# Two-input work on GpSimd and VectorE in planned turns, weight sums on VectorE, one decay operation per batch row

## The chip, the cores and the metric

The kernel runs on one core of a Trainium2 chip. The core has five engines that run on their own instruction queues, each strictly in order: TensorE (PE in the profile, with its weight loads as PEld), VectorE (DVE), ScalarE (ACT), GpSimd (POOL) and SyncE (SP, which here only issues DMAs). They wait for each other through semaphores. [...] The metric is the device time of one execution in microseconds (us), given as the median of several runs. The profile is of one further execution.

## The reference

A gated linear attention is followed by a mixture of four experts, all of which see every token:

```python
B, H, S, D = 4, 8, 768, 48
f = 1.0 / (1.0 + np.exp(-f_logit))
for t in range(S):
    state = f[:, :, t, :, None] * state + np.einsum('bhd,bhe->bhde', k[:, :, t], v[:, :, t])
    y[:, :, t] = np.einsum('bhd,bhde->bhe', q[:, :, t], state)
x = y.transpose(0, 2, 1, 3).reshape(B * S, H * D)              # 3072 x 384
p = domain_probs / (domain_probs.sum(-1, keepdims=True) + 1e-09)
for e in range(4):                                             # w1: 384 x 1024, w2: 1024 x 384
    h = np.maximum(x @ w1[e], 0.0)
    out += p[:, e:e + 1] * (h @ w2[e])
```

## The kernel before

**Tiling.** The 768 steps are cut into six chunks `c` of 128 (0 to 5), each with four batch rows `b`, so a chunk is 512 tokens. In names, "q 3.1" is the step `q` of chunk 3, batch row 1; "relu 2.0.6.0" is chunk 2, expert 0, slice 6 of the 1024 hidden columns, from token column 0.

**Attention of a chunk.** The gates' logarithms are summed along the chunk by a matmul. ScalarE takes two exponentials of the sums (`exps`, into a tile `e`; there are two such tiles). `product` (L298) multiplies q and k with them into a tile `qk`: on VectorE for the first chunks, on GpSimd from chunk 1, batch row 2 on. A transposing DMA (or, early, PE) makes `QK` of it; PE multiplies to scores `A`, VectorE masks them (`ev_at`, L338: one input in PSUM, the mask in SBUF), PE makes `y`. `cast_v` (L303) casts v for it, mostly on GpSimd. Between chunks a state is carried: VectorE adds PE's product to `Sf` (`ev_kv`, L362), and `state` (L364) on GpSimd multiplies `Sf` by the chunk's decay `egs` and casts the result to `Sb`. The state lies in two bands of 48 partitions (0 to 47 and 64 to 111), one for each head of a pair; the partitions between the two hold zero. From chunk 1 on `egs` is fetched by a DMA that GpSimd's queue issues (L296), reading from the last row of tile `e`; this tile is free for a next chunk's `exps` when this DMA and both products have read it.

**Experts.** y, scaled by the expert's probability from chunk 2 on (`ev_x`, ScalarE L318 or VectorE L320), is transposed by DMA to `xT`. PE makes h (L386), ScalarE or VectorE applies the relu while it leaves PSUM (`relu`, L395 and L397). In chunks 0 and 1, PE multiplies h with w2 (L401), and VectorE adds the experts up (`ev_o`, L408). From chunk 2 on the second product is made by two experts at a time and in blocks of two by two, with seven products instead of eight (`p1` to `p7`, L447). For this, four block sums of each h are needed, s1 to s4 (`h_sum`, L435, 128 x 1024 bf16, all on VectorE; s3 overwrites a block of h), and four block differences of each w2 (`w_sum`, L424, 128 x 768 bf16, j = 0 to 3; j = 1 overwrites a block of w2, so an expert's `w_sum` comes after the last plain product with its w2, in chunk 1). Before the change experts 0, 2 and 3 have theirs on GpSimd and expert 1 on VectorE. The seven products are combined in SBUF (`add_c`, L454): first with what PSUM holds, then sums of two SBUF tiles (`plus`, L683), on VectorE or GpSimd.

**What sets the order.** The program's order on every engine is written by a planner, `Plan.run` (L59). Each step has engines on which it may run with a cost in us, a priority, steps it depends on, and buffers it takes and frees. The planner walks through time, gives each free engine the ready step with the first priority, and lists the steps in the order of their planned starts; this list is then emitted. So any change to a cost or to a rule moves steps on all engines, and moves some between engines (a relu between ScalarE and VectorE, for example). On the chip the order on each engine is fixed, while the time of each step is what the semaphores allow.

## Time and profile before

| | |
|---|---|
| median of 3 runs | 317.05 us (315.5 to 317.67) |
| profiled execution, its own time | 315.88 us |
| its span, first to last instruction | 313.9 us |
| mean granted TensorE clock | 0.974 |
| PE busy | 283.7 us (90% of the span) |
| VectorE busy | 206.2 us (66%) |
| ScalarE busy | 182.9 us (58%) |
| GpSimd busy | 141.9 us (45%) |

The span leaves 2.0 us of the profiled execution outside of it. An instruction counts as busy from its start to its end, so the time in which it has started and cannot go on is in it too. The granted clock is the share of TensorE's full clock that the chip allows at that time. Rows with "gap" or "[... <-X]" say how long an engine was idle and what ended this.

### The profile page before, as it was taken

The numbers are of one execution on the slowest core, as the hardware profiler recorded it, in microseconds if no ns is written. First come the engines' busy times: TensorE is split into PE (matmuls) and PEld (weight loads), VectorE is DVE, ScalarE is ACT, GpSimd is POOL, SyncE is SP. The second block draws the span as 40 slices with busy tenths as digits, with TensorE's granted clock in tenths as the row PEclk, the third lists the DMA queues.
The fourth block names the chain that finished last, engine by engine and source line by source line (L and its number), as shares of the span: only waits on it lengthen the run. The fifth ranks groups of instructions, "written<-read, shape, count | busy, mean of one in ns | idle before, by whom it ended". The sixth has DMA issues, their size and how long they took to land.

```text
span 313.9 us, 6483 instructions
## 1 busy us (share of the span) xinstructions
PE 283.7 (90%) x2519; PEld 195.3 (62%) x2548; DVE 206.2 (66%) x340; ACT 182.9 (58%) x347; POOL 141.9 (45%) x199
## 2 busy tenths in 40 slices
PE   6999999999988799923999998998899997999993
PEld 2566555677766564413777766767567766667693
DVE  3874025864653676999789698587998377450363
ACT  5766737476746558820668486757556661656520
POOL 3877102291858919994087463653960001010012
PEclk9999999999999979995899999999999999999998
DMA  8999999969895978990287999796444424110002
GB/s 157 192 190 208 205 206 187 207 164 172 160 202 111 170 145 140 232 199 16 56 160 145 211 204 159 144 146 88 82 94 106 80 18 84 45 58 0 2 12 90
DMA packets 157330, 41.20 MB, mean 131 GB/s; under 512 B 145756, under 2 KB 156508, under 8 KB 157300
## 3 DMA queue, kind: packets, MB, share of 16 engines
q1 hardware_dynamic: 146052, 34.07, 58.0%
q0 software_dynamic: 11248, 6.72, 14.8%
q8 instruction: 20, 0.33, 0.5%
q14 instruction: 10, 0.08, 0.1%
HBM read 31.51 MB, written 4.72 MB: 115 GB/s over the span
## 4 chain that ended last, share of the span: by engine, by line
PE 47%; DMA 20%; DVE 10%; POOL 10%; issue 7%; ACT 3%; SPq 2%; DVEq 0%; POOLq 0%; ACTq 0%
PE ps L386 21%; PE ps L447 19%; DMA w_sb<-in_moe_w_dram 10%; DVE s L435 4%; POOL qk L299 4%; PE ps L401 4%; DMA k<-in_k_dram 3%; DMA xT<-yb 3%; DVE h L435 2%; SPq L234 2%; POOL w_sb L243 2%; ACT yb L318 2%; DVE yb L320 2%; DMA QK<-qk 2%; DMA egs<-e 1%
## 5 line engine op out<-in xcount | busy, mean ns | idle before, releaser
L386 PE MATMUL ps<-xT,w_sb 128*128 128x512 bf16 (+3 forms) x679 | 142.3, 339 | 2.3 <-DVE Sf L362 0.4
L397 ACT ACTIVATE h<-ps 128x512 bf16<-128x512 f32 (+2 forms) x182 | 97.0, 544 | 54.9 <-PE ps L386 50.5
L386 PEld LDWEIGHTS <-w_sb 128*128 128x128 bf16 x708 | 65.8, 98 | 47.0 <-issue 1.0
L447 PEld LDWEIGHTS <-h 128*128 128x128 bf16 x512 | 43.9, 99 | 18.9 <-issue 11.3
L401 PE MATMUL ps<-w_sb,h 128*128 128x384 bf16 x256 | 51.4, 331 | 2.2 <-ACT e L291 1.8
L454 POOL TENSOR_TENSOR o<-o,o 128x384 f32<-128x384 f32 x8 | 8.3, 1044 | 72.1 <-DVE o L454 41.3
L369 POOL TENSOR_TENSOR Sf<-Sf,egs 48x192 f32<-48x192 f32 x40 | 21.8, 545 | 38.7 <-DVE Sf L362 24.8
L447 PEld LDWEIGHTS <-s 128*128 128x128 bf16 x384 | 32.2, 98 | 6.3 <-DVE s L435 2.0
L401 PEld LDWEIGHTS <-h 128*128 128x128 bf16 x256 | 24.8, 99 | 17.8 <-issue 2.8
L447 PE MATMUL ps<-w_sb,h 128*128 128x192 bf16 x256 | 24.8, 253 | 12.1 <-DVE h L395 12.1
L395 DVE TENSOR_SCALAR h<-ps 128x256 bf16<-128x256 f32 (+2 forms) x46 | 24.3, 545 | 15.9 <-PE ps L386 15.2
L291 ACT ACTIVATE e<-ps 128x384 f32<-128x384 f32 x48 | 26.9, 666 | 11.0 <-DMA egs<-e 3.7
L338 DVE TENSOR_TENSOR AT<-ps,mask 128x512 bf16<-128x512 f32 x48 | 30.3, 683 | 3.2 <-PE ps L334 3.2
L408 DVE SCALAR_TENSOR_TENSOR o<-ps,pn,o 128x384 f32<-128x384 f32 x24 | 14.6, 615 | 26.7 <-PE ps L401 26.2
L435 DVE TENSOR_TENSOR s<-h 128x1024 bf16<-128x1024 bf16 x16 | 18.7, 1168 | 16.7 <-ACT h L397 16.6
L320 DVE TENSOR_SCALAR yb<-ps,pn 128x384 bf16<-128x384 f32 x27 | 16.4, 616 | 19.6 <-ACT yb L318 14.2
L299 POOL TENSOR_TENSOR qk<-q,e 128x384 bf16<-128x384 f32 x18 | 22.8, 1270 | 13.4 <-ACT e L291 12.2
L318 ACT ACTIVATE yb<-ps,pn 128x384 bf16<-128x384 f32 x37 | 20.5, 582 | 13.3 <-DVE yb L320 10.4
L299 POOL TENSOR_TENSOR qk<-k,e 128x384 bf16<-128x384 f32 x20 | 22.6, 1135 | 8.7 <-ACT e L291 4.3
L454 DVE TENSOR_TENSOR o<-o,ps 128x384 f32<-128x384 f32 (+1 forms) x36 | 18.8, 538 | 11.2 <-PE ps L447 8.3
L223 ACT COPY o<-ps 128x384 f32<-128x384 f32 x23 | 11.0, 479 | 23.5 <-PE ps L447 23.4
L447 PE MATMUL ps<-w_sb,s 128*128 128x192 bf16 x256 | 23.9, 246 | 0.0
(74 smaller groups left out, 335.4 us busy)
## 6 DMA issues: line engine op xcount, KB each, us to landing
out_dram<-o SPq DMA_DIRECT2D x23, 192.0 KB, 2.0
w_sb<-in_moe_w_dram POOLq DMA_DIRECT2D x5, 768.0 KB, 18.1
k<-in_k_dram SPq DMA_DIRECT2D x10, 384.0 KB, 5.2
q<-in_q_dram SPq DMA_DIRECT2D x10, 384.0 KB, 5.1
v<-in_v_dram SPq DMA_DIRECT2D x10, 384.0 KB, 5.1
f<-in_f_logit_dram SPq DMA_DIRECT2D x9, 384.0 KB, 4.6
w_sb<-in_moe_w_dram POOLq DMA_DIRECT2D x6, 384.0 KB, 8.4
f<-in_f_logit_dram SPq DMA_DIRECT2D x6, 192.0 KB, 3.8
```

The costliest lines, as they stand in the source:

```text
L291: nc.scalar.activation(out=o, in_=i, func=AF.Exp, scale=1.0 if j else -1.0)
L299: engines[eng].tensor_tensor(out=tl("qk", c, b)[:, j, :, 0:D].rearrange("t (i r) d -> t i r d", r=2), in0=tl("qk"[j], c, b // 2)[:, hh(b), ...
L318: nc.scalar.activation(out=out, in_=in_, func=AF.Copy, scale=pe)
L320: nc.vector.tensor_single_scalar(out=out, in_=in_, scalar=pe, op=ALU.mult)
L338: nc.vector.tensor_tensor(out=tl("AT", c, b)[:, r], in0=tl("A", c, b, r), in1=mask01.unsqueeze(1).broadcast_to([T, NP, T]), op=ALU.mult)
L386: nc.tensor.matmul(out=hp(c, e, fc, n0, n1, nf)[:, f], lhsT=w1_sb[:, e, kk, (fc + f) * 128:(fc + f + 1) * 128], rhs=x_of(c, e)[:, kk, n0:n ...
L395: nc.vector.tensor_relu(out=dst, in_=src)
L397: nc.scalar.activation(out=dst, in_=src, func=AF.Relu)
L401: nc.tensor.matmul(out=tl("op", c, e, nt, part)[:, cols], lhsT=tl("h", c, e, half_of(c, nt * T))[:, fc, nt * T:(nt + 1) * T], rhs=w2_sb[:, ...
L435: engines[eng].tensor_tensor(out=o, in0=x, in1=y, op=op)
L447: nc.tensor.matmul(out=tl("pp_", c, g, bank(c, g, r))[:, u], lhsT=a[:, fc, u * T:(u + 1) * T], rhs=w[:, fc], start=(n + fc == 0 and bank(c ...
L454: engines[eng].tensor_tensor(out=o[:, us], in0=x[:, us], in1=y[:, us], op=ALU.add)
```

## The change

Three things are changed.

1. Steps that read SBUF on GpSimd, and steps with two SBUF inputs on VectorE, are marked `port`: the products of chunks 1 to 5, `cast_v`, `state`, `w_sum`, `h_sum`, and the sums of two SBUF tiles (`plus`). The planner starts no marked step on either engine while another marked one is planned to run. Where a marked GpSimd step follows a marked VectorE step in this order, it gets a semaphore wait for it (`behind`); 24 GpSimd steps get one. VectorE gets no wait for GpSimd.
2. All sixteen `w_sum` steps are on VectorE, planned at 0.62 us each; before, twelve were on GpSimd, planned at 1.75 us.
3. `state` makes one decay multiplication over partitions 0 to 111 instead of one for each band; the two casts stay. Its planned cost goes from 1.75 to 1.25 us.

The helpers `copy`, `product`, `cast_v`, `w_sum`, `h_sum`, `add_c` now return the instruction they make, so that a wait can be put on it; line numbers move by three to six.

```diff
@@ Plan.run
+        port, last = 0.0, None
...
-                        if e in o.costs:
+                        if e in o.costs and not (o.port and e in ("DVE", "POOL") and port > now + 1e-9):
...
+                    if o.port and e in ("DVE", "POOL"):
+                        if e == "POOL" and last is not None and last.engine == "DVE":
+                            o.behind = last
+                        port, last = o.end, o
...
-            nexts = [t for t in free_at.values()] + [f[0] for f in freeing]
+            nexts = [t for t in free_at.values()] + [f[0] for f in freeing] + [port]
@@ state
-        egs, nb = tl("egs", c, b)[:, 0:NP], Sb
+        eg = tl("egs", c, b)[0:MP, 0:NP].unsqueeze(2).broadcast_to([MP, NP, D])
+        first = nc.gpsimd.tensor_tensor(out=Sf[:, b], in0=Sf[:, b], in1=eg, op=ALU.mult)
         for r in range(2):
             rows = slice(r * P2, r * P2 + D)
-            eg = egs[rows, :].unsqueeze(2).broadcast_to([D, NP, D])
-            nc.gpsimd.tensor_tensor(out=Sf[rows, b], in0=Sf[rows, b], in1=eg, op=ALU.mult)
-            nc.gpsimd.tensor_copy(out=nb[rows, b, :, r * D:(r + 1) * D], in_=Sf[rows, b])
+            nc.gpsimd.tensor_copy(out=Sb[rows, b, :, r * D:(r + 1) * D], in_=Sf[rows, b])
+        return first
@@ attention (port=c > 0 for the products, port=True for cast_v)
-            kvdone[c, b] = P.add(f"state {c}.{b}", {"POOL": 1.75}, on(state), s15 + 0.2,
-                                 deps=[ek, GS[b]], frees=[("egs", c, b)])
+            kvdone[c, b] = P.add(f"state {c}.{b}", {"POOL": 1.25}, on(state), s15 + 0.2,
+                                 deps=[ek, GS[b]], frees=[("egs", c, b)], port=True)
@@ add_wsum (add_sums and plus: port=True, costs as they were)
-            wsum[e] = P.add(f"w_sum{j} {e}", {"DVE": 0.62} if e == 1 else {"POOL": 1.75}, lambda eg, j=j: w_sum(e, j, eg), unit[0] + 6,
-                            deps=[omm[c, e, nt] for c in range(S0) for nt in range(B)] + [wsum.get(e)])
+            wsum[e] = P.add(f"w_sum{j} {e}", {"DVE": 0.62}, lambda eg, j=j: w_sum(e, j, eg), unit[0] + 6,
+                            deps=[omm[c, e, nt] for c in range(S0) for nt in range(B)] + [wsum.get(e)], port=True)
@@ the emission
-        o.emit(o.engine)
+        o.made = o.emit(o.engine)
+        if o.behind is not None:
+            after(o.made, o.behind.made)
```

The order that the planner makes of it differs at many places. On VectorE, between the last `ev_o` of chunk 1 and the first block sums of chunk 2 (the numbers in the names are buffers; `w_sb` and `tw` are written by the weight sums, `h` by the relus, `s` by the block sums, `yb` by the scaling of y), the order before is:

```order
125 L408 SCALAR_TENSOR_TENSOR o_1472<-ps_1701,pn,o_1472 128x384
126 L408 SCALAR_TENSOR_TENSOR o_1523<-ps_1750,pn,o_1523 128x384
127 L320 TENSOR_SCALAR yb_1831<-ps_1766,pn 128x384
128 L424 TENSOR_TENSOR w_sb<-w_sb 128x4x192
129 L424 TENSOR_TENSOR tw<-w_sb 128x768
130 L408 SCALAR_TENSOR_TENSOR o_1472<-ps_1824,pn,o_1472 128x384
131 L424 TENSOR_TENSOR tw<-w_sb,tw 128x768
132 L408 SCALAR_TENSOR_TENSOR o_1523<-ps_1833,pn,o_1523 128x384
133 L395 TENSOR_SCALAR h_1880<-ps_1910 128x512
134 L395 TENSOR_SCALAR h_1880<-ps_1915 128x512
135 L395 TENSOR_SCALAR h_1935<-ps_1924 128x512
136 L435 TENSOR_TENSOR s_1944<-h_1880 128x1024
```

With the change the same stretch (w_sum is L429 there, the relu L400, the block sum L440) is:

```order
128 L400 TENSOR_SCALAR h_1700<-ps_1807 128x256
129 L429 TENSOR_TENSOR tw<-w_sb 128x768 x2
130 L429 TENSOR_TENSOR w_sb<-w_sb 128x4x192
131 L413 SCALAR_TENSOR_TENSOR o_1465<-ps_1813,pn,o_1465 128x384
132 L413 SCALAR_TENSOR_TENSOR o_1515<-ps_1822,pn,o_1515 128x384
133 L429 TENSOR_TENSOR tw<-w_sb 128x768
134 L429 TENSOR_TENSOR w_sb<-w_sb 128x4x192
135 L429 TENSOR_TENSOR tw<-w_sb,tw 128x768
136 L429 TENSOR_TENSOR tw<-w_sb 128x768 x2
137 L429 TENSOR_TENSOR tw<-w_sb,tw 128x768
138 L400 TENSOR_SCALAR h_1863<-ps_1894 128x512
141 L440 TENSOR_TENSOR s_1937<-h_1863 128x1024
```

Nine weight sums stand ahead of the relu of slice 6 (row 133 before, 138 now), where three stood; between rows 138 and 141 are the two other relus. Two small relus, rows 126 and 128 of the change, have come from ScalarE.

On GpSimd, in the same time, the order before has the products and casts of chunk 3 (`qk`, `vb`), the DMA issues of the decays (`egs`) and the weight sums without a wait for VectorE between them ("Activation", "DMAHW" and "Pool" are semaphores of ScalarE, of a load and of GpSimd itself):

```order
114 L296 DMA egs_1908<-e_100 128x1x4
115 L296 DMA egs_1919<-e_102 128x1x4
116 L424 TENSOR_TENSOR tw<-w_sb 128x768 x2
117 L424 TENSOR_TENSOR w_sb<-w_sb 128x4x192 [waits Pool_49]
118 L299 TENSOR_TENSOR qk_98<-q_1898,e_100 128x8x48 [waits DMAHW7_49,DMAHW1_49,Activation_49]
119 L299 TENSOR_TENSOR qk_98<-k_1878,e_100 128x8x48 [waits DMAHW0_49,Activation_49]
120 L225 CAST vb_2026<-v_1937 128x384 [waits DMAHW3_49]
121 L299 TENSOR_TENSOR qk_90<-q_1898,e_102 128x8x48 [waits Activation_49]
122 L299 TENSOR_TENSOR qk_90<-k_1878,e_102 128x8x48 [waits Activation_49]
123 L225 CAST vb_2082<-v_1937 128x384
```

With the change the products of batch rows 0 and 1 of chunk 3 stand in this form:

```order
91 L301 DMA egs_1838<-e_100 128x1x4 [waits Activation_49]
92 L304 TENSOR_TENSOR qk_94<-q_1696,e_100 128x8x48 [waits DMAHW2_49,DVE_49,Pool_49]
93 L304 TENSOR_TENSOR qk_94<-k_1518,e_100 128x8x48 [waits DMAHW4_49,Activation_49]
94 L301 DMA egs_1870<-e_102 128x1x4 [waits Activation_49]
95 L230 CAST vb_1907<-v_1749 128x384 [waits DMAHW3_49,DVE_49]
96 L304 TENSOR_TENSOR qk_96<-q_1696,e_102 128x8x48 [waits DMAHW6_49]
97 L304 TENSOR_TENSOR qk_96<-k_1518,e_102 128x8x48 [waits Activation_49]
```

The weight sums are gone from it; row 92 waits for the third weight sum on VectorE (row 130 there), row 95 for the ninth (row 137). Later in the queue the cast "v 3.1" waits for s1 2.0, "q 3.2" for s4 2.0 and "k 3.2" for a weight sum of expert 2.

On GpSimd in chunk 2, the DMA issue of the first decay (egs 2.0, row 64) stood ahead of the products before:

```order
64 L296 DMA egs_1207<-e_100 128x1x4 [waits DMASW3_49,Activation_49]
65 L299 TENSOR_TENSOR qk_96<-k_1114,e_100 128x8x48 [waits DMAHW5_49,Activation_49]
66 L299 TENSOR_TENSOR qk_98<-k_1114,e_102 128x8x48 [waits Activation_49]
67 L299 TENSOR_TENSOR qk_96<-q_1145,e_100 128x8x48 [waits DMAHW6_49]
68 L369 TENSOR_TENSOR Sf<-Sf,egs_1081 48x192 [waits DMASW1_49,DVE_49]
69 L370 CAST sb<-Sf 48x4x48 [waits PE_49,Pool_49]
70 L369 TENSOR_TENSOR Sf<-Sf,egs_1081 48x192 [waits DVE_49]
```

With the change it stands at the end of this group, next to the second (egs 2.1, row 70):

```order
59 L371 TENSOR_TENSOR Sf<-Sf,egs_1066 112x192 [waits DMASW1_49,DVE_49]
60 L374 CAST sb<-Sf 48x4x48 [waits PE_49,Pool_49]
61 L374 CAST sb<-Sf 48x4x48
62 L371 TENSOR_TENSOR Sf<-Sf,egs_1079 112x192 [waits DMASW2_49,DVE_49,Pool_49]
63 L374 CAST sb<-Sf 48x4x48 [waits PE_49,Pool_49]
64 L374 CAST sb<-Sf 48x4x48
65 L304 TENSOR_TENSOR qk_96<-q_1137,e_100 128x8x48 [waits DMAHW6_49,Pool_49]
66 L230 CAST vb_1321<-v_1176 128x384 [waits DMAHW7_49]
67 L304 TENSOR_TENSOR qk_98<-q_1137,e_102 128x8x48
68 L230 CAST vb_1353<-v_1176 128x384
69 L301 DMA egs_1356<-e_100 128x1x4 [waits DMASW3_49]
70 L301 DMA egs_1375<-e_102 128x1x4 [waits DMASW4_49]
```

The two states of chunk 1 (rows 68 to 75 before, 59 to 64 now) have gone ahead of the q products, and both decays' fetches come last.

More of the change, by code (lines that the diff above doesn't have):

```diff
@@ L21, in __init__ @@
         self.takes, self.frees, self.lag = list(takes), list(frees), lag
-        self.end = self.start = self.engine = None
+        self.end = self.start = self.engine = self.behind = None
+        self.port = port
         self.pad = 0
@@ L222, in copy @@
         if eng == "ACT":
[L223 to L225 removed]
+            return nc.scalar.copy(out=out, in_=in_)
+        return engines[eng].tensor_copy(out=out, in_=in_)
     def load(c, nm, b, n):
@@ L451, in add_c @@
         if x is None:
-            copy(eng, o[:, us], y[:, us])
-        else:
-            engines[eng].tensor_tensor(out=o[:, us], in0=x[:, us], in1=y[:, us], op=ALU.add)
+            return copy(eng, o[:, us], y[:, us])
+        return engines[eng].tensor_tensor(out=o[:, us], in0=x[:, us], in1=y[:, us], op=ALU.add)
     def store_c(c, i, j, o, us):
```

29 lines of the change are left out of this document (13 added, 16 removed).

## The prediction

> **What bounds the kernel now.** I read the page's slices first, then stretches of 8 us around the gap in them, then the chain of waits through the gap, then the one line that the chain names. On the page, each digit is the busy tenths of a fortieth of the span:
>
> ```profile
> PE   6999999999988799923999998998899997999993
> ```
>
> PE is full nearly everywhere except in slices 18 and 19, and in the tail. Stretches around them (busy us and count per engine, then the granted clock):
>
> ```profile
> core 0: us, PE busy (x) PEld busy (x) DVE busy (x) ACT busy (x) POOL busy (x), PEclk, DMA share, GB/s
> 136.00:144.00 8.00, 0.00 (x0) 0.00 (x0) 8.00 (x2) 0.33 (x1) 7.98 (x8) 0.79 0.78 149
> 144.00:152.00 8.00, 5.54 (x46) 4.33 (x47) 7.97 (x13) 1.25 (x3) 0.42 (x1) 0.57 0.01 2
> 152.00:160.00 8.00, 7.95 (x102) 5.94 (x101) 5.51 (x12) 6.00 (x12) 3.25 (x8) 1.00 0.56 107
> ```
>
> From 136 to 144 PE does nothing, and VectorE is "busy" for 8.00 us with parts of two instructions. The chain of waits (start, us, what) and the list of who waited for whom (us, times, longest) show the connection:
>
> ```profile
> 128.22 6.55 DVE s L435
> 134.80 2.97 DVE s L435
> 137.77 7.21 DVE h L435
> ...
> 146.24 2.71 PE ps L447 x16
> 148.96 0.97 PE ps L334 x16
> ...
> 151.19 1.32 PE ps L447 x16
> 152.51 0.65 PE ps L386 x3
> ...
> 158.85 0.55 PE ps L334 x16
> ```
>
> ```profile
> PE ps L447 <- DVE h L395: 12.1, 2, 10.5
> ```
>
> PE waited 10.5 us for relus that stand on VectorE behind three block sums. Such a sum is short elsewhere (ns, min/median/max):
>
> ```profile
> L435 DVE TENSOR_TENSOR s<-h x16: 677/692/6542, 128.2 to 300.2; 128x1024 bf16<-128x1024 bf16 x16
> ...
> L435 DVE TENSOR_TENSOR h<-h x16: 677/686/7292, 137.7 to 302.0; 128x1024 bf16<-128x1024 bf16 x16
> ```
>
> The maxima are two of the three in the chain. Together these took 6.55 + 2.97 + 7.29 = 16.8 us for work of 3 x 0.69 = 2.1, so 14.7 us of standing. What GpSimd did then, in order of time:
>
> ```profile
> 128.22 3.24 POOL L424 TENSOR_TENSOR tw<-w_sb 128x768 bf16<-128x768 bf16 x2
> 131.41 1.64 POOL L424 TENSOR_TENSOR w_sb<-w_sb 128x768 bf16<-128x768 bf16 x1
> 133.01 1.18 POOL L299 TENSOR_TENSOR qk<-q,e 128x384 bf16<-128x384 f32 x1
> 134.15 1.47 POOL L299 TENSOR_TENSOR qk<-k,e 128x384 bf16<-128x384 f32 x1
> 135.57 0.49 POOL L225 CAST vb<-v 128x384 bf16<-128x384 f32 x1
> ...
> 139.61 1.65 POOL L424 TENSOR_TENSOR tw<-w_sb 128x768 bf16<-128x768 bf16 x1
> ...
> 142.79 1.63 POOL L424 TENSOR_TENSOR tw<-w_sb,tw 128x768 bf16<-128x768 bf16 x1
> ```
>
> A row that starts before the last one's end, as at 134.15, belongs to one train with it. The first sum starts with the train of weight sums at 128.22 and ends at 134.8, only after three of them and the q product. The third ends at 145.0, right after the last weight sum (144.4). So VectorE is shut out while a train lasts, not for one instruction. It gets a turn between a q and a k product: there the k product takes 1.47 us instead of
>
> ```profile
> L299 POOL TENSOR_TENSOR qk<-k,e x20: 988/1012/1465, 6.3 to 230.8; 128x384 bf16<-128x384 f32 x20
> ```
>
> its 1.01.
>
> **The change part by part.** *The hole.* The weight sums leave GpSimd, so the trains that made the hole are gone: 10.5 us of PE idle time. Behind it PE ran at a granted clock of 0.57: sixteen L447 matmuls took 2.71 us against 1.32 at 151.19, and sixteen L334 ones 0.97 against 0.55, so 1.39 + 0.42 = 1.8 us more. Both go if PE does not stop: -12.3.
>
> The Trainium skill ("SBUF — State Buffer", section "Who interferes with whom") says that the pair of SBUF ports that VectorE and GpSimd share is locked for one whole instruction, and that a VectorE instruction with two SBUF inputs meets a GpSimd one that reads SBUF. By that rule three sums lose at most 4.9 us, and the change is worth little (a rival, below). The trace agrees on who collides and not on how long: 14.7 us.
>
> *What VectorE takes over.* Its own three weight sums of before give the price:
>
> ```profile
> 120.04 0.58 DVE L424 TENSOR_TENSOR w_sb<-w_sb 128x768 bf16<-128x768 bf16 x1
> 120.66 0.75 DVE L424 TENSOR_TENSOR tw<-w_sb 128x768 bf16<-128x768 bf16 x1
> ...
> 121.86 0.73 DVE L424 TENSOR_TENSOR tw<-w_sb,tw 128x768 bf16<-128x768 bf16 x1
> ```
>
> Mean 0.69 us. Ahead of the relu of slice 6, nine stand where three stood: 6 x 0.69 = 4.1 us, and two relus of 128x256 from ScalarE at 0.42 (group below): 0.8. VectorE had idled 3.2 us there, waiting for PE:
>
> ```profile
> 118.46 1.14 DVE L408 SCALAR_TENSOR_TENSOR o<-ps,pn,o 128x384 f32<-128x384 f32 x2
> 126.32 1.99 DVE L395 TENSOR_SCALAR h<-ps 128x512 bf16<-128x512 f32 x3 [3.20 <-PE ps L386]
> L395 DVE TENSOR_SCALAR h<-ps 128x256 bf16<-128x256 f32 x24 | 9.8, 422 | 10.2 <-PE ps L386 9.7 <-ACT h L397 0.3
> ```
>
> So the relus come 4.9 - 3.2 = 1.7 us late. Collisions add to it: the q and k products of "q 3.0" start behind the third weight sum and last 1.2 + 1.0 us; two `ev_o` (1.14 us), which read PSUM, cover half, so the next weight sum stands between 0 and 2.2 us; I take 1.0, one turn, because turns pass between products. Up to the score masks of chunk 3, two more weight sums (1.4) come and one relu of 0.66 (1.99 for three) goes: +0.7. Five more follow by the block sums of expert 2: 3.4 us, and VectorE had 2.5 us idle in 152 to 160, so 0 to 3.4 lands on PE; I take 1.0. Together +4.4, between 2.4 (1.7 + 0.7) and 8.0.
>
> *The decay.* 128x384 on GpSimd takes 1.01 us, 48x192 takes 0.50 (the median of the group below), half for half the elements of a partition, so I take 0.5 for 112x192 too; if rows counted, it would be up to 1.0 and nothing gained. A state saves 0.5 and a step of 0.08:
>
> ```profile
> L369 POOL TENSOR_TENSOR Sf<-Sf,egs x40: 495/502/1047, 25.0 to 220.9; 48x192 f32<-48x192 f32 x40
> L296 POOL DMA_DIRECT2D egs<-e x16 | 9.0, 563 | 11.2 <-ACT e L291 11.2
> 89.10 4.56 DMA egs<-e
> 93.76 1.16 ACT L291 ACTIVATE e<-ps 128x384 f32<-128x384 f32 x2 [3.70 <-DMA egs<-e]
> 94.98 0.81 PE L401 MATMUL ps<-w_sb,h 128*128 128x384 bf16 x4 [1.83 <-ACT e L291]
> ```
>
> Here it is on the path: ScalarE waited 3.70 us for the decay's fetch (egs 2.1), relus stood behind, and PE stood 1.83 us. Two states ahead of this issue give 2 x 0.58 = 1.15 us. The issue of egs 2.0 (0.56 us) goes from the front of the group to its end, just ahead of this one; so the whole group starts 0.5 us earlier, egs 2.0 is issued at 89.1 - 1.15 - 0.5 = 87.5, and egs 2.1 at 88.0. But the earlier pair of `exps` waits now for the late egs 2.0, on ScalarE, in front of the same relus: after a fetch of 4.56 us it starts at 92.1, and the second pair ends at 94.3 (1.1 us each) instead of 94.9. I take -0.6, bounds -1.15 and +1.2 (one pair's 1.16 us behind the last landing). The other eighteen states are off the path.
>
> *Later collisions.* In chunk 4, PE waited for a block sum that ran 1.52 us instead of 0.69, beside the product "q 5.0":
>
> ```profile
> 217.46 1.20 POOL L299 TENSOR_TENSOR qk<-q,e 128x384 bf16<-128x384 f32 x1 [0.83 <-POOL sb L370]
> 217.68 1.52 DVE s L435
> PE ps L447 <- DVE s L435: 1.8, 1, 1.8
> ```
>
> "q 5.0" now waits for a later VectorE step: -0.8, bounds 0 and -1.8.
>
> *The waits.* Behind a waiting GpSimd instruction stand products, casts and decay fetches; the transposing DMAs and then PE's scores wait for those. The longest such chain: "k 3.2" waits for a weight sum of expert 2, which VectorE ends at 129.0 (126.3 + 2.7) + five relus 3.3 + eight block sums 5.5 + two weight sums 1.4 = 139.2. "k 3.3" ends 3.7 us behind that (1.0 + 0.5 + 1.2 + 1.0), and a transpose takes up to
>
> ```profile
> 189.70 4.74 DMA QK<-qk
> ```
>
> 4.74 us: 147.6. PE reached these scores (L334) at 158.85, without the hole and its slow clock at 146.5; but they now stand behind five more h groups of 0.65 and one p5 of 1.32: 151.1. Cover of 3.5 us, so 0; without it every us of VectorE's lag counts here again.
>
> Sum: 315.88 - 12.3 + 4.4 - 0.6 - 0.8 = 306.6. The profiled execution lies 1.2 us below the median of the runs, 317.05; I add some of that and say 307.
>
> **The rivals.** *VectorE becomes the bound.* It is 7.97 of 8 us busy behind the hole. If the costs reach their bound of 8.0 and nothing else is gained, the sum is 315.9 - 12.3 + 8.0 = 311.6. For: thirteen more weight sums stand ahead of s4 of expert 2 than in this stretch before. Against: several stand where VectorE was idle. Chance 0.17.
>
> *The hole is only filled otherwise.* GpSimd keeps trains of products and casts: the third sum was shut out through a k product, a cast and a fetch too. If "q/k 3.0", "q/k 3.1 and cast" and "k 3.2 to cast 3.3" (2.2, 2.7 and 4.2 us) each catch a two-input step for their whole length, 9.1 of the 14.7 us return, as PE's wait, beside 4.4: 315.9 - 12.3 + 9.1 + 4.4 = 317.1. Against: turns pass between products, and these trains lie beside masks that read PSUM. Chance 0.12.
>
> *One instruction at a time.* If a sum is shut out for one GpSimd instruction only, at most 1.65 us, three lose 4.9 us; the hole then has another cause, which stays, and the time is 315.9 - 4.9 + 4.4 = 315.4. Against: 14.7 us in one piece with the trains. Chance 0.03. This is what the Trainium skill's rule above would do here.
>
> *The turns chain the two queues, slower.* From chunk 4's first cast on, seventeen GpSimd steps wait for a VectorE step where none did. If PE waits one product, 1.2 us, for each, that costs 20 us; from the eighth on (8 x 1.2 = 9.6) the gain is gone, and at twelve the time is 306.6 + 14.4 = 321. For: SyncE waited for GpSimd's products 11.3 us in total already:
>
> ```profile
> SPq L312 <- POOL qk L299: 11.3, 7, 5.2
> ```
>
> Against: GpSimd is 45% busy and its products lead the scores by several us. Chance 0.11.
>
> *More is won:* VectorE's slack takes nearly all, the costs stay at 2.4 and the later collisions give 1.8: 315.9 - 12.3 + 2.4 - 1.8 - 1.2 = 303. Chance 0.07 for below that.
>
> **How the numbers follow.** Forecast (303 to 311): 0.50; more 0.07; VectorE bound 0.17; filled otherwise 0.12 and one instruction at a time 0.03; slower 0.11. A measurement of this kernel tells about 1% from no change, 313.9 to 320.2 around the median. Faster: 0.50 + 0.07 + 0.17 = 0.74; same 0.12 + 0.03 = 0.15; slower 0.11. The range goes from 302 (most of "more" is inside) to 316 (the least of "filled otherwise"), with some 0.2 left out: 0.03 below, slower's 0.11, and about half of "filled otherwise".
>
> **What would show it.** Right: no L435 above 2.5 us; no PE gap above 3 us between 120 and 160; a clock above 0.9 there; sixteen L424 on VectorE, most under 1 us; twenty decay operations near 0.5 us with 112 rows. Wrong: L424 or L435 on VectorE at 2 to 4 us beside products; PE waiting for L400 by 3 us or more near 128; "PE <- DMA QK" in chunks 3 to 5; decays of 1 us. The forecast falls if PE's idle time in the whole stretch from 100 to 160 shrinks by less than 5 us.

## The result, and the profile after

| | before | after |
|---|---|---|
| median of the runs | 317.05 us (315.5 to 317.67) | 300.53 us (299.31 to 300.63) |
| profiled execution, its own time | 315.88 us | 299.31 us |
| its span | 313.9 us | 297.4 us |
| mean granted TensorE clock | 0.974 | 0.996 |
| PE busy | 283.7 us | 280.5 us (94%) |
| VectorE busy | 206.2 us | 186.1 us (63%) |
| GpSimd busy | 141.9 us | 107.4 us (36%) |

The ratio is 0.9476, with a 95% interval from 0.9411 to 0.9542. The changed kernel is 5% faster, and with 300.53 us it lies below the low end of the predicted range (302). The direction was forecast, and so was the mechanism that bounded the kernel before; the size was not, and neither was what the waits are worth. The profiled execution of experiment 1 below ran 4 us longer than the median of its kernel's runs, so only lengths of single instructions and what waited for what are read from it.

The page of the changed kernel, its span and two rows of the slices:

```profile
span 297.4 us, 6465 instructions
...
PE   7999999999997979999998999999999969999992
...
PEclk9999999999999999999999999999999999999998
```

The two slices in which PE had stood are full, and the clock is granted throughout. The stretches of 8 us around the former hole (busy us and count for PE, PEld, DVE, ACT and POOL, then clock, DMA share, GB/s):

```profile
136.00:144.00 8.00, 7.95 (x95) 6.35 (x94) 5.93 (x12) 5.63 (x10) 5.30 (x11) 1.00 0.99 183
144.00:152.00 8.00, 7.95 (x84) 5.47 (x84) 6.96 (x13) 5.47 (x11) 1.27 (x3) 1.00 0.91 176
```

Where VectorE was "busy" for 8.00 us with parts of two instructions, it now is for 5.93 us with twelve. The operations that had stood, and the ones that moved, each in the view of its own line (count, ns min/median/max, first and last start):

```profile
L440 DVE TENSOR_TENSOR s<-h x16: 679/692/1506, 126.7 to 283.6; 128x1024 bf16<-128x1024 bf16 x16
...
L440 DVE TENSOR_TENSOR h<-h x16: 678/683/685, 129.3 to 285.3; 128x1024 bf16<-128x1024 bf16 x16
...
L429 DVE TENSOR_TENSOR tw<-w_sb x8: 543/550/1226, 118.1 to 147.2; 128x768 bf16<-128x768 bf16 x8
...
L371 POOL TENSOR_TENSOR Sf<-Sf,egs x20: 495/506/953, 25.7 to 207.8; 112x192 f32<-112x192 f32 x20
```

No block sum lasts more than 1.51 us (7.29 before), and the decay over 112 rows takes what the one over 48 took.

To see where the 16.6 us between the two profiled executions came from, I compare the times at which PE starts the weight load of the n-th matmul of the second product (`p`, L447 before, L452 after). The order on PE is nearly the same in both, so the difference at each point is what has been won so far:

```
p matmul     before us   after us   won so far
0             132.70      130.42       2.28
64            156.50      141.35      15.15
192           181.51      167.60      13.92
384           218.23      202.37      15.86
448           237.06      219.05      18.02
640           273.03      256.39      16.64
895 (last)    308.44      291.80      16.64
```

So 2.3 us are won ahead of the hole, 12.9 us across it, and 1.5 us net behind it. The 2.3 us ahead of it show in PE's stretches (busy us and count, then clock, DMA share, GB/s). Before:

```profile
100.00:112.00 12.00, 10.05 (x103) 0.92 1.02 162
112.00:160.00 48.00, 36.66 (x302) 0.88 0.69 133
```

After:

```profile
100.00:112.00 12.00, 10.12 (x123) 1.00 1.00 161
112.00:160.00 48.00, 46.83 (x424) 1.00 0.94 184
```

In the 60 us from 100 to 160, PE's idle time fell from 13.3 to 3.1 us, and the clock rose. In 100 to 112 PE is as busy as before, yet it starts 123 matmuls instead of 103. In part these are shorter ones, and in part it is the clock: before, it was 0.75 in 108 to 112 and 0.83 in 112 to 116, which makes 4 x (0.25 + 0.17) = 1.7 us, and after it is 1.00 in both.

What is left of PE's waits (us, times, longest):

```profile
PE ps L452 <- DVE h L400: 2.3, 1, 2.3
...
PE ps L391 <- DVE yb L325: 1.6, 1, 1.6
```

Neither has to do with VectorE standing; both lead to the same buffer, as experiment 8 shows.

### The profile page after: what moved, and what is told of

Read it like the earlier page. It is cut to its first block, busy times and chain, and to the rows that moved or that the text cites. A ratio compares the mean times of both kernels' runs of the same rounds, so it can differ in the third digit from the quotient of the medians.

```text
span 297.4 us, 6465 instructions
## 1 busy us (share of the span) xinstructions
PE 280.5 (94%) x2520; PEld 193.9 (65%) x2548; DVE 186.1 (63%) x350; ACT 182.5 (61%) x347; POOL 107.4 (36%) x169
## 3 DMA queue, kind: packets, MB, share of 16 engines
q0 software_dynamic: 11248, 6.72, 15.9%
## 4 chain that ended last, share of the span: by engine, by line
PE 78%; DMA 7%; DVE 4%; ACT 3%; SPq 2%; issue 2%; POOL 2%; DVEq 0%; ACTq 0%; POOLq 0%
PE ps L391 38%; PE ps L452 21%; PE ps L406 12%; DMA xT<-yb 4%; SPq L239 2%; PE ps L339 2%; ACT yb L323 2%; DVE yb L325 2%; DMA q<-in_q_dram 2%; DMA egs<-e 1%; PE ps L354 1%; DVE AT L343 1%; POOL qk L304 1%; PE ps L350 1%; PE ps L360 1%
## 5 line engine op out<-in xcount | busy, mean ns | idle before, releaser
L391 PE MATMUL ps<-xT,w_sb 128*128 128x512 bf16 (+3 forms) x680 | 140.1, 338 | 4.7 <-ACT e L296 1.7
L406 PE MATMUL ps<-w_sb,h 128*128 128x384 bf16 x256 | 50.1, 326 | 0.1
L452 PEld LDWEIGHTS <-h 128*128 128x128 bf16 x512 | 42.6, 98 | 7.5 <-DVE h L400 2.5
L452 PEld LDWEIGHTS <-s 128*128 128x128 bf16 x384 | 32.1, 98 | 4.7 <-DVE s L440 0.5
L458 POOL TENSOR_TENSOR o<-o,o 128x384 f32<-128x384 f32 x11 | 10.9, 994 | 65.2 <-DVE o L458 54.0
L406 PEld LDWEIGHTS <-h 128*128 128x128 bf16 x256 | 24.4, 98 | 15.2 <-DVE yb L325 0.2
L325 DVE TENSOR_SCALAR yb<-ps,pn 128x384 bf16<-128x384 f32 x29 | 17.6, 616 | 19.8 <-ACT yb L323 15.0
L400 DVE TENSOR_SCALAR h<-ps 128x256 bf16<-128x256 f32 (+2 forms) x43 | 22.2, 529 | 12.5 <-PE ps L391 11.6
L304 POOL TENSOR_TENSOR qk<-k,e 128x384 bf16<-128x384 f32 x20 | 20.5, 1026 | 25.2 <-ACT e L296 13.2
L452 PE MATMUL ps<-w_sb,h 128*128 128x192 bf16 x256 | 23.6, 246 | 2.3 <-DVE h L400 2.3
L371 POOL TENSOR_TENSOR Sf<-Sf,egs 112x192 f32<-112x192 f32 x20 | 10.5, 527 | 38.9 <-DVE Sf L367 18.0
L452 PE MATMUL ps<-w_sb,s 128*128 128x192 bf16 x256 | 24.1, 246 | 0.0
L452 PE MATMUL ps<-tw,h 128*128 128x192 bf16 x256 | 23.6, 246 | 0.0
L440 DVE TENSOR_TENSOR s<-h 128x1024 bf16<-128x1024 bf16 x16 | 12.8, 799 | 16.6 <-ACT h L402 16.4
```

The lines of the kernel that those rows point to most:

```text
L304: return engines[eng].tensor_tensor(out=tl("qk", c, b)[:, j, :, 0:D].rearrange("t (i r) d -> t i r d", r=2), in0=tl("qk"[j], c, b // 2)[:, ...
L325: nc.vector.tensor_single_scalar(out=out, in_=in_, scalar=pe, op=ALU.mult)
L391: nc.tensor.matmul(out=hp(c, e, fc, n0, n1, nf)[:, f], lhsT=w1_sb[:, e, kk, (fc + f) * 128:(fc + f + 1) * 128], rhs=x_of(c, e)[:, kk, n0:n ...
L400: nc.vector.tensor_relu(out=dst, in_=src)
L406: nc.tensor.matmul(out=tl("op", c, e, nt, part)[:, cols], lhsT=tl("h", c, e, half_of(c, nt * T))[:, fc, nt * T:(nt + 1) * T], rhs=w2_sb[:, ...
L452: nc.tensor.matmul(out=tl("pp_", c, g, bank(c, g, r))[:, u], lhsT=a[:, fc, u * T:(u + 1) * T], rhs=w[:, fc], start=(n + fc == 0 and bank(c ...
```

## The experiments

Two theories stood against each other at first: that the weight sums on GpSimd were the trouble and their move was the gain (the forecast, with the waits at nothing), or that the planned order and its waits do more than that. "Stands" in the table is the time, summed over VectorE's operations with two SBUF inputs (none from PSUM, where PE's products lie; the early products of q and k are not counted), by which each lasted longer than the shortest of the same line, tiles and shape (where over 0.15 us). "Own" means that GpSimd steps wait for the GpSimd step ahead of them. The kernel before was run again beside each group of experiments (medians 317.46, 316.41 and 316.22 us), and each ratio is to the runs beside it. All of these kernels compute the whole result, and nothing is left out.

Experiments 2, 6, 9 and 10 keep the order of the changed kernel's steps on every engine, experiment 4 keeps that of the kernel before, and experiment 7 that of experiment 1. In experiments 1, 3 and 5 the planner writes a new order, so these measure their edit and the order together.

| kernel | sums on VectorE | planned turns | waits | decay in one | us, median | ratio to before (95%) | stands, us |
|---|---|---|---|---|---|---|---|
| before | 4 of 16 | no | no | no | 317.05 | 1 | 25.8 |
| 1 sums alone | 16 | no | no | no | 308.88 | 0.977 (0.968 to 0.986) | 16.4 |
| 2 no waits | 16 | yes | no | yes | 307.07 | 0.972 (0.964 to 0.979) | 15.9 |
| 3 sums on GpSimd | 4 | yes | yes | yes | 314.5 | 0.996 (0.989 to 1.004) | 4.1 |
| 4 no trains | 4 | no | own | no | 309.82 | 0.983 (0.974 to 0.993) | 20.9 |
| 5 decay alone | 4 | no | no | yes | 310.9 | 0.983 (0.976 to 0.990) | 21.1 |
| 6 both ways | 16 | yes | both ways | yes | 300.02 | 0.947 (0.943 to 0.951) | 0 |
| 7 sums, no trains | 16 | no | own | no | 306.96 | 0.971 (0.966 to 0.976) | 15.7 |
| 8 fourth buffer | 16 | yes | yes | yes | 296.26 | 0.937 (0.932 to 0.942) | 2.7 |
| 9 two decays | 16 | yes | yes | no | 301.35 | 0.954 (0.949 to 0.959) | 4.7 |
| 10 more sums | 16 + 8 | yes | yes | yes | 302.8 | 0.960 (0.953 to 0.966) | 3.3 |
| after | 16 | yes | yes | yes | 300.53 | 0.948 (0.941 to 0.954) | 4.0 |

**1. The weight sums alone.** The kernel before, with one edit:

```diff
-            wsum[e] = P.add(f"w_sum{j} {e}", {"DVE": 0.62} if e == 1 else {"POOL": 1.75}, ...
+            wsum[e] = P.add(f"w_sum{j} {e}", {"DVE": 0.62}, ...
```

> The kernel before, with all sixteen weight sums on VectorE at a planned 0.62 us; no port rule, no waits, the decay as before. Theory A (trains: VectorE is shut out as long as GpSimd instructions follow each other without a gap, and the long trains were the weight sums): the stop of 10.5 us is gone, the longest block sum is below 3.5 us, and most of the gain is here: 301 to 305 us. Theory B (turns: the port rule and its waits, which keep two-input work apart, make the gain): products and casts still collide with the sums, 308 to 314 us, with a stop of 3 us or more between 120 and 160.

Measured: 308.88 us (307.56 to 312.81), so 8 of the 16.5 us. That is theory B's range, though the stop of 3 us or more that theory B expected did not come: the longest between 120 and 160 is 1.7 us. The views of the block sums and weight sums, and PE's longest waits:

```profile
L435 DVE TENSOR_TENSOR h<-h x16: 678/685/1681, 133.6 to 298.9; 128x1024 bf16<-128x1024 bf16 x16
...
L424 DVE TENSOR_TENSOR tw<-w_sb x8: 543/778/1548, 111.0 to 136.0; 128x768 bf16<-128x768 bf16 x8
```

```profile
PE ps L349 <- DVE AT L338: 2.4, 3, 1.7
PE ps L447 <- DVE s L435: 2.4, 1, 2.4
```

No block sum exceeds 1.7 us, so the large hole is gone with the weight sums. But half of the weight sums of this form now take 0.78 us or more, beside products and casts, and PE waits for masks and block sums in pieces of 2 us. Moving the sums is not the whole gain.

**2. The changed kernel without its 24 waits.** The order that the planner wrote stays.

```diff
         o.made = o.emit(o.engine)
-        if o.behind is not None:
-            after(o.made, o.behind.made)
```

> The changed kernel in the same order, without the 24 waits of GpSimd steps for VectorE steps. Theory A: the waits are worth nothing or little, 299 to 302 us; some sums stand 1 to 2 us for a product, off PE's path. Theory B: 304 to 312 us, with VectorE's two-input steps standing 8 us or more in total instead of 4.0.

Measured: 307.07 us (305.35 to 307.65). That is theory B's range. By the medians the waits are worth 6.5 us. Between the two profiled executions PE falls 8.3 us behind: 1.4 of it at the stop at 107, behind which the clock falls to 0.59 here and stays at 1.00 in the changed kernel (nothing shows that to be a matter of the waits), and 5.4 between 122 and 140. The order of time on GpSimd and on VectorE (start us, us), near the place of the former hole:

```profile
133.26 1.01 POOL L304 TENSOR_TENSOR qk<-k,e 128x384 bf16<-128x384 f32 x1
134.20 0.51 POOL L230 CAST vb<-v 128x384 bf16<-128x384 f32 x1
134.67 1.19 POOL L304 TENSOR_TENSOR qk<-q,e 128x384 bf16<-128x384 f32 x1
135.82 0.98 POOL L304 TENSOR_TENSOR qk<-k,e 128x384 bf16<-128x384 f32 x1
136.76 0.49 POOL L230 CAST vb<-v 128x384 bf16<-128x384 f32 x1
```

```profile
133.19 4.61 DVE L440 TENSOR_TENSOR h<-h 128x1024 bf16<-128x1024 bf16 x1
137.72 0.68 DVE L440 TENSOR_TENSOR s<-h,s 128x1024 bf16<-128x1024 bf16 x1
...
138.32 0.68 DVE L400 TENSOR_SCALAR h<-ps 128x512 bf16<-128x512 f32 x1
```

```profile
PE ps L452 <- DVE h L400: 4.4, 2, 2.4
```

A block sum of 0.68 us starts 0.07 us ahead of the k product and ends 0.55 us behind the last cast of the train. It got no turn in five GpSimd instructions, among them a q and a k product in a row; the relu behind it was late, and PE waited for that. A weight sum at 124.42 lasted 3.68 us in the same way. The changed kernel has the same five steps on GpSimd and holds the first of them back by a wait:

```profile
135.24 0.99 POOL L304 TENSOR_TENSOR qk<-k,e 128x384 bf16<-128x384 f32 x1 [2.86 <-DVE tw L429]
```

GpSimd waits 2.86 us until VectorE is through, and PE has no gap of 0.2 us behind it until 157.57.

**3. The turns without the move.** The changed kernel, with the weight sums of experts 0, 2 and 3 on GpSimd again:

```diff
-            wsum[e] = P.add(f"w_sum{j} {e}", {"DVE": 0.62}, ...
+            wsum[e] = P.add(f"w_sum{j} {e}", {"DVE": 0.62} if e == 1 else {"POOL": 1.75}, ...
```

> The changed kernel, with the weight sums of experts 0, 2 and 3 back on GpSimd at a planned 1.75 us; port rule, waits and the one decay stay. Theory A: trains of weight sums are on GpSimd again; the plan sets them apart from VectorE's block sums, but VectorE has no wait, so where the real times differ from the plan it is shut out for 3 us or more at least once: 305 to 313 us. Theory B: the turns are enough, 300 to 304 us, no block sum above 2.5 us.

Measured: 314.5 us (313.68 to 315.45), no difference from before that this run can tell, and outside both ranges: no stand of 3 us came, as theory A had it, and no gain, as theory B had it. PE's longest waits:

```profile
PE ps L452 <- DVE h L440: 2.8, 1, 2.8
PE ps L452 <- DVE s L440: 2.5, 1, 2.5
```

VectorE stands for only 4.1 us, as in the changed kernel, and yet nothing is won: with twelve weight sums of 1.64 us on GpSimd, each of which keeps VectorE's two-input steps out by plan, block sums come late: the seventh starts at 150.56 us, in the changed kernel at 133.40, and PE stands 2.8 us for it. As far as this order shows, the collisions have become waits, and the turns pay only once the long steps have left GpSimd.

**4. The kernel before, with its trains broken.** Order and engines stay; each product, cast, state, weight sum and sum of two tiles on GpSimd waits for the end of the one before it on GpSimd, so that there is a short gap between them:

```diff
-        o.emit(o.engine)
+        made = o.emit(o.engine)
+        if o.engine == "POOL" and ...:      # product, cast, state, w_sum, plus
+            first, last = made if isinstance(made, tuple) else (made, made)
+            if before_it is not None:
+                after(first, before_it)
+            before_it = last
```

> The kernel before in the same order, on the same engines, where every product, cast, state, weight sum and sum of two tiles on GpSimd also waits for the end of the GpSimd step before it, so that none starts before the other's end. Theory A: between two GpSimd steps VectorE gets its turn, a block sum takes at most 0.69 + 1.65 = 2.3 us (3 at most), the stop of 10.5 us shrinks below 3 us and the low clock behind it goes: 303 to 308 us, although no work has moved. If VectorE is shut out for the sake of the load on GpSimd, not of the missing gap, nothing changes: 315 to 319 us, block sums of 6 to 7 us.

Measured: 309.82 us (308.97 to 313.08). The stop and the clock did what theory A expected; the time lies above its range of 303 to 308.

```profile
L436 DVE TENSOR_TENSOR s<-h x16: 682/725/2775, 127.8 to 293.2; 128x1024 bf16<-128x1024 bf16 x16
...
L436 DVE TENSOR_TENSOR h<-h x16: 677/686/2130, 132.6 to 294.9; 128x1024 bf16<-128x1024 bf16 x16
```

No work moved, and the two sums of 6.5 and 7.3 us are down to 2.8 and 2.1, each now ending in the gap behind one weight sum (the first spans the issue of a fetch too). PE's stop of 10.5 us became two of 1.65 and 2.85 (the longest gaps between its matmuls), and the clock stays at 1.00 there. In total VectorE still stands 20.9 us of 25.8, in shorter pieces: what cost most was the length of a stand at the place where PE waited, not the sum. This is the plainest evidence for the forecast's mechanism: what shut VectorE out was the missing gap between GpSimd's steps.

**5. The decay alone.** The kernel before, with the new `state` and its planned cost of 1.25.

```diff
-        egs, nb = tl("egs", c, b)[:, 0:NP], Sb
+        eg = tl("egs", c, b)[0:MP, 0:NP].unsqueeze(2).broadcast_to([MP, NP, D])
+        nc.gpsimd.tensor_tensor(out=Sf[:, b], in0=Sf[:, b], in1=eg, op=ALU.mult)
...
-            kvdone[c, b] = P.add(f"state {c}.{b}", {"POOL": 1.75}, on(state), s15 + 0.2,
+            kvdone[c, b] = P.add(f"state {c}.{b}", {"POOL": 1.25}, on(state), s15 + 0.2,
```

> The kernel before with the one decay operation for all partitions (planned at 1.25 us instead of 1.75), nothing else. If the decay is worth only what it saves on GpSimd's path at 89 us: the stop of 10.5 us or one like it stays, 315 to 318 us. If the shorter states move the products out of the weight sums' train by another plan: below 313 us.

Measured: 310.9 us (309.57 to 313.64), ratio 0.983, the second of the two ranges. VectorE in order of time around the hole:

```profile
130.33 4.40 DVE L434 TENSOR_TENSOR h<-h 128x1024 bf16<-128x1024 bf16 x1
...
141.74 3.87 DVE L434 TENSOR_TENSOR s<-h,s 128x1024 bf16<-128x1024 bf16 x1
```

Two stands of 4.4 and 3.9 us are left of 6.5, 3.0 and 7.2. The new planned cost gave another order, in which products and casts lie between the weight sums. So this is, as far as the trace shows, a gain of the order: 5 to 6 us for a planned cost that is 0.5 us smaller. What the shorter decay itself is worth is experiment 9.

**6. Waits in both directions.** In the changed kernel VectorE's marked steps also wait for the marked GpSimd step ahead of them in the plan:

```diff
-                        if e == "POOL" and last is not None and last.engine == "DVE":
+                        if last is not None and last.engine != e:
```

> The changed kernel, where a marked VectorE step behind a marked GpSimd step in the plan's order also waits for it (for the first instruction of a state). If turns in one direction do all: VectorE's standing of 4.0 us only becomes waiting, 299.5 to 303 us, slower where VectorE waits for a GpSimd step that comes later than planned. If the other direction is missing: 296 to 299 us and no two-input step on VectorE above 1 us.

Measured: 300.02 us (299.39 to 300.38).

```profile
L440 DVE TENSOR_TENSOR s<-h x16: 684/692/728, 128.1 to 284.6; 128x1024 bf16<-128x1024 bf16 x16
...
L440 DVE TENSOR_TENSOR h<-h x16: 680/685/693, 130.0 to 286.3; 128x1024 bf16<-128x1024 bf16 x16
```

Nothing stands any more, and the time is that of the changed kernel, in the first of the two ranges. The 4.0 us that VectorE still stood there cost nothing that these runs can tell, and neither do the further waits.

**7. The move and broken trains, without a plan.** Edits 1 and 4 together on the kernel before.

> The kernel before with the weight sums on VectorE (as in the first run of this list) and with every marked GpSimd step also waiting for the end of the GpSimd step before it (as in the fourth); the planner knows no turns. If short gaps on GpSimd are all that the turns give: 299 to 303 us. If the order that keeps two-input steps apart is needed, VectorE still stands 10 us or more in total, for one GpSimd step each: 304 to 309 us.

Measured: 306.96 us (306.48 to 309.13), only some 2 us below experiment 1 and 6.4 above the changed kernel. PE's longest waits:

```profile
PE ps L448 <- DVE s L436: 2.5, 1, 2.5
PE ps L348 <- DVE AT L337: 2.5, 3, 1.7
```

The time is in the second range. With gaps everywhere each stand is one GpSimd step, but there are many (15.7 us), as in experiment 2. The last 6 us need more than gaps. Which of the planned order, its waits and the shorter decay brings them, this kernel does not separate; experiment 2 says that the order and the shorter decay without the waits do not (307.07 us).

**8. A fourth buffer for `yb`.** The waits that are left in the changed kernel lead to `yb`, the scaled y, which a step frees only when its transposing DMA is through. VectorE in order of time:

```profile
244.14 0.62 DVE L325 TENSOR_SCALAR yb<-ps,pn 128x384 bf16<-128x384 f32 x1 [2.33 <-DMA xT<-yb]
244.67 0.68 DVE L400 TENSOR_SCALAR h<-ps 128x512 bf16<-128x512 f32 x1
```

The relu for which PE waits 2.3 us stands behind a step that waits 2.33 us for the third `yb`. One `vb` buffer makes the room:

```diff
-             "vb": 6, ..., "yb": 3, ...
+             "vb": 5, ..., "yb": 4, ...
```

> The changed kernel with four buffers for yb instead of three (and five instead of six for vb, to make room). PE's stops of 1.6 us at 107 and 2.3 us at 243 end behind a scaling of y into yb that had waited for a transpose by DMA. If the third buffer is their cause, both are gone or halved: 296 to 298.5 us. If it is the DMA's length itself: 299.5 to 302 us.

Measured: 296.26 us (296.08 to 297.67), ratio 0.937 to the kernel before: it beats both kernels. PE's longest waits:

```profile
PE ps L276 <- ACT gp L272: 1.7, 2, 1.0
...
PE ps L391 <- ACT yb L323: 0.5, 1, 0.5
```

The wait of 2.3 us is gone, and the one of 1.6 us for `yb` is down to 0.5, as the first range had it. Between the two profiled executions the place at 243 brings 2.4 us and the one at 107 1.8, of which 1.5 are lost again by 136. The planner also moved two steps from VectorE to ScalarE, which this kernel does not separate from the buffers.

**9. The changed kernel with the decay in two operations.** Order, engines and waits stay.

```diff
-        first = nc.gpsimd.tensor_tensor(out=Sf[:, b], in0=Sf[:, b], in1=eg, op=ALU.mult)
         for r in range(2):
             rows = slice(r * P2, r * P2 + D)
+            eg = egs[rows, :].unsqueeze(2).broadcast_to([D, NP, D])
+            m = nc.gpsimd.tensor_tensor(out=Sf[rows, b], in0=Sf[rows, b], in1=eg, op=ALU.mult)
```

> The changed kernel with the decay in two operations of 48x192 as before; order, engines and waits are the changed kernel's, so twenty states take 0.58 us longer on GpSimd than the order counts with. Theory A (the forecast's term: -0.6, all of it from the fetch of egs at 89 to 94, the eighteen other states off the path): 300.8 to 301.5, the gap of PE near 92 longer by 0.3 to 1.0 us. Theory B (with the waits, a longer state also delays what waits behind it on both engines): 302 to 305, with new gaps of PE after 120. Theory C (GpSimd has the room everywhere): within 0.3 of the changed kernel.

Measured: 301.35 us (300.44 to 303.0). That is in the first theory's range, but the interval of its ratio (0.949 to 0.959) overlaps the changed kernel's, so the times alone do not separate it from no difference. The traces show where it would come from. The fetch of egs and ScalarE's `exps` behind it, with two decays:

```profile
90.21 3.85 DMA egs<-e
...
94.16 2.23 ACT L296 ACTIVATE e<-ps 128x384 f32<-128x384 f32 x4 [4.43 <-DMA egs<-e]
```

In the changed kernel:

```profile
88.58 4.19 DMA egs<-e
...
92.88 2.23 ACT L296 ACTIVATE e<-ps 128x384 f32<-128x384 f32 x4 [3.65 <-DMA egs<-e]
```

The fetch starts 1.6 us earlier with one decay (1.2 of it are two states of 0.58; PE was 0.5 us late ahead of this already), and PE's gap there is 1.69 us instead of 2.48 long. So the shorter decay is worth about 0.8 us at this one place.

**10. More work for VectorE.** The changed kernel, with the first and the last weight sum of each expert issued twice, which adds eight operations:

```diff
-        return engines[eg].tensor_tensor(out=o, in0=x, in1=y, op=ALU.subtract)
+        for _ in range(2 if j in (0, 3) else 1):
+            made = engines[eng].tensor_tensor(out=o, in0=x, in1=y, op=ALU.subtract)
+        return made
```

> The changed kernel, but of each expert's four weight sums the first and the last are issued twice in a row on VectorE (the second writes the same values), so VectorE does eight more operations of 128x768, 8 x 0.47 to 0.55 = 3.8 to 4.4 us, in 118 to 148 us, in the same order. Theory A (the forecast's term of +4.4: VectorE has little room there, so what it takes over lands on PE nearly in full): 303.5 to 305.5, with PE waiting for relus near 128 and for block or weight sums behind. Theory B (VectorE has the room, work that it takes over costs PE nothing so long as nothing shuts it out): 300 to 301.5, no PE gap above 0.5 us in 118 to 150.

Measured: 302.8 us (302.31 to 305.14), between the two ranges, so neither theory holds as it was put. The comparison of PE's milestones with the changed kernel says more than the total: this execution is 0.57 us late ahead of the weight sums already, 1.6 us at p matmul 64 and 2.2 us at 192. So the eight operations, 3.8 us of work, cost PE some 1.6 us, in many idle pieces, the longest of 0.40 us. (Another 1.5 us come at 245 to 260, where the granted clock is 0.89; the weight sums are long done by then.) VectorE had room for what was moved there, but not for much more.

## Why the prediction was right and wrong

**Right: what bounded the kernel, and what the change does to it.** The hole and the slow clock behind it were put at -12.3; across this place PE won 12.9. Experiment 4 shows the mechanism by itself: the same work on the same engines loses its long stands as soon as there are gaps between GpSimd's steps. The signs that were named came as named: no block sum above 2.5 us (longest 1.51), no PE gap above 3 us between 120 and 160 (longest 0.8), a clock of 1.00 there, sixteen weight sums on VectorE of which most are under 1 us, twenty decays of 0.5 us. PE's idle time from 100 to 160 shrank by 10.2 us where 5 were asked for.

**Wrong: the term of +4.4 us for what VectorE takes over.** It measured about nothing: the 12.9 us across the hole are net, and PE has no gap of 0.2 us or more between the stop of 1.59 us at 107.28 and one of 0.80 us at 157.57. The order of time on VectorE shows why:

```profile
118.12 1.02 DVE L429 TENSOR_TENSOR tw<-w_sb 128x768 bf16<-128x768 bf16 x2
119.05 0.55 DVE L429 TENSOR_TENSOR w_sb<-w_sb 128x768 bf16<-128x768 bf16 x1
...
120.58 1.23 DVE L429 TENSOR_TENSOR tw<-w_sb 128x768 bf16<-128x768 bf16 x1
121.73 1.35 DVE L429 TENSOR_TENSOR w_sb<-w_sb 128x768 bf16<-128x768 bf16 x1
123.00 0.54 DVE L429 TENSOR_TENSOR tw<-w_sb,tw 128x768 bf16<-128x768 bf16 x1
...
124.88 1.87 DVE L400 TENSOR_SCALAR h<-ps 128x512 bf16<-128x512 f32 x3
```

Three things were mis-sized. The price of 0.69 us was a duration taken from sums that stood themselves; undisturbed ones start 0.47 us apart (118.12, then the third at 119.05), so six cost 2.8 us and not 4.1. The two collisions with a q and a k product came (0.68 and 0.80 us too long, 1.5 together where I took 1.0). The relu of slice 6 starts at 124.88, 1.44 us earlier than before, while PE is 2.28 us ahead: 0.84 us late against PE instead of 1.7 and more, and this much PE did not feel. And the seven weight sums behind, for which 0.7 and 1.0 us were taken, left no gap of 0.2 us in PE. The room is not unlimited: in experiment 10 eight more operations cost 1.6 us.

**Wrong: the waits at nothing.** The forecast asked only what the waits might cost and found cover of 3.5 us. That part held: GpSimd waits up to 3.4 us for a block sum, and the one wait of PE that GpSimd ends, in the whole execution, is 0.2 us. But the waits also win: without them the time is 307.07 us (experiment 2). The forecast, which gave the waits neither cost nor gain, said 307 for a kernel like that one, and that it meets the number is luck. Across the hole experiment 2 wins 8.7 us where -12.3 + 4.4 = -7.9 was forecast, but what it lacks against 12.9 is lost to stands of 3.7 and 4.6 us and the stops behind them, and not to the price of the moved sums. The reading behind it was that trains of products are harmless, "because turns pass between products". Experiment 2 shows a stand of 4.61 us in a train of products and casts. The rival "the hole is only filled otherwise" had this right as a mechanism; it would have come true in part had the change not had its waits. But the forecast had it as a way to lose, and gave the waits no gain for stopping it.

**Not foreseen: 2.3 us ahead of the hole.** Behind a stop of 1.71 us at 107.42, PE had run at a reduced clock (0.92 in the mean from 100 to 112, and 0.83 from 112 to 116), which by the working above makes 1.7 of the 2.3 us. After the change a stop of 1.59 us stands at the same place, and the clock stays at 1.00. The forecast looked at the slow clock behind the large hole alone. I did not test what decides this, and the slow clock can come back: in experiment 2, with the changed kernel's order, the stop at this place is 1.73 us long and the clock behind it 0.59. So this part is not shown to be the change's doing, and may be luck.

**The decay, -0.6.** The decays take 0.5 us as estimated, and experiment 9 finds about 0.8 us for them in the changed order. Against the kernel before, PE's stop at this place shrank only by 0.14 us (1.83 to 1.69): the fetch starts at 88.58 and not at 87.5. From the first k product to the fetch the group is 1.0 us shorter, close to the 1.15 that were forecast for two states. But it starts at 80.59 instead of 80.07, where 79.5 was forecast, because it waits for the `exps` ahead of it, which come later in ScalarE's new order. Before, then after:

```profile
78.35 2.28 ACT L291 ACTIVATE e<-ps 128x384 f32<-128x384 f32 x4 [1.14 <-PE ps L271]
...
79.30 2.28 ACT L296 ACTIVATE e<-ps 128x384 f32<-128x384 f32 x4 [0.48 <-PE ps L276]
```

The term was right for the operation and wrong for this change.

**The later collisions, -0.8.** From p matmul 64 on 1.5 us are won net: up to 2.9 by p matmul 448, of which 1.4 are given back in the wait for `yb` at 243.

**The rivals.** VectorE did not become the bound: in 136 to 144 it is 5.93 of 8 us busy. The turns did not chain the queues: PE waited 0.2 us for GpSimd. "One instruction at a time" fell with experiments 2 and 4. "More is won" came about, below 303, but not for its reason: it kept a cost of 2.4 us for VectorE and left the waits at nothing.

Together: -2.3 ahead of the hole, -12.9 across it and -1.5 behind it make -16.7, for 16.6 measured between the two profiled executions; the forecast had -9.3. Of the 7.4 us between them, 5.0 are the term of VectorE's work (-12.3 + 4.4 against -12.9), 1.7 the stretch ahead of the hole less the decay, and 0.7 the later part. The 5.0 us and the 6.5 of the waits are not two gains: across the hole, the kernel without the waits lacks 4.2 us of the 12.9. So the two steps that failed are one. The forecast priced VectorE's new work by operations that stood, and did not see that the waits keep it from standing.

## What to carry to other kernels

When two engines hinder each other, ask of each wait between them what it prevents as well as what it costs, and price it against the run without it: here 24 waits that looked free were 6.5 us of gain. The parts of such a change don't add up: the move alone gave 8 us, the turns and the decay without the move next to nothing, the decay alone 5 to 6 through another order, and all three 16.5. Where a planner rewrites the order with every edit, only an experiment that keeps the order tells what an edit is worth. And take the price of a moved operation from the distance of undisturbed starts, not from the mean duration of ones that stood.

## What the runs showed of the hardware

**When VectorE gets its turn.** Over six traces (before, after, and experiments 1 to 4) I looked at the places where an operation of VectorE with two SBUF inputs (one that stood 0.3 us or more in all) was still standing when a GpSimd step ended. Where the next GpSimd step started 60 to 200 ns later, VectorE got its turn 26 times of 26. Where it started before the recorded end of the last one, it did so 28 times of 47: 15 of 18 from a q to a k product, but 5 of 10 from a k product to a cast, 1 of 5 from a cast to a q product, and in none of 4 between two weight sums. Behind the issue of an egs fetch, with the next step within 60 ns, it got none in 8. So in these traces a turn was sure only with a gap. Why the chance differs between the pairs, these runs don't show. The Trainium skill ("SBUF — State Buffer", "Who interferes with whom") has the shared port pair as a lock that is held for one instruction; the stands of 4.61 us over five instructions and of 7.3 us before last longer than that, those of experiment 4 do not: there, with gaps, nothing stands for more than one computing step.

**The clock behind short stops.** PE's clock fell behind stops that were much shorter than the large one, and not each time. With two decays (experiment 9), behind a stop of 2.48 us at 92.9 and one of 1.60 us at 109.8 (PE, PEld, DVE, ACT, POOL, then clock, DMA share, GB/s):

```profile
96.00:100.00 4.00, 4.00 (x22) 2.53 (x21) 0.42 (x1) 1.86 (x7) 3.94 (x5) 0.65 0.04 8
...
112.00:116.00 4.00, 3.96 (x30) 2.56 (x28) 2.96 (x6) 2.04 (x6) 0.00 (x0) 0.57 0.77 155
```

In the changed kernel, stops of 1.69 and 1.59 us at the same places have 1.00 behind them. The length alone does not decide it: behind a stop of 2.12 us at 242.7 in experiment 6 the clock is 0.59 in 244 to 248, behind one of 2.29 us at 243.1 in the changed kernel it is 1.00. So a stop of 1.6 us can cost some 1.5 us more than itself, or nothing, and a forecast for a kernel with such stops carries this much uncertainty for each.
